# Forward V of heads 1 to 30 in one transfer per head, one product tile instead of two, V of head 30 kept for the backward

## The chip, the cores and the metric

The kernel runs on one core of a Trainium2 chip. The metric is the device time of one execution in microseconds (us). Engine names are those of the profile: PE is the matrix engine, PEld its weight loads, DVE the vector engine, ACT the scalar engine, POOL the general engine, SP the engine whose queue issues most transfers. A transfer is carried by 16 DMA engines, each with a share of its rows. The three runs of the kernel before lie within 3.2 us of each other.

## The reference

The forward is an adaptive layer norm block: an attention with one query token against a cache of 32 heads x 8192 keys x 192, and then a small mixer MLP, each gated by a modulation vector. The kernel computes the output and the gradients of nine inputs, the whole K and V cache among them.

```python
mod = silu(c) @ w_mod                       # six vectors of 640: sa, ca, ga, sb, cb, gb
h = layernorm(x) * (1 + ca) + sa
x = x + ga * attention(h, k_cache, v_cache, wq, wo)
h = layernorm(x) * (1 + cb) + sb
x = x + gb * mixer_mlp(h, w1, w2, w3, w4)

def attention(x, k, v, wq, wo):             # 1 token, 32 heads, 8192 keys, 192 wide
    q = (x @ wq) split in heads
    p = softmax(q . k * 192 ** -0.5)
    return (p . v, heads joined) @ wo

# returned: x, and by jax.vjp(grad_out) the gradients of
# x, k_cache, v_cache, wq, wo, w3, w4, c, w_mod
```

For a head with output gradient do, the backward needs dV = p x do (an outer product of 8192 x 192), dP = V . do, dS = p * (dP - c), and dK = dS x q (again an outer product).

## The kernel before, in words

**Tiles.** A head's K or V is laid out with 64 rows on each of the 128 partitions. It is handled in two halves, t = 0 and 1: a half tile is 128 partitions x 32 rows x 192 numbers of 2 bytes, that is 12288 bytes per partition, 1536 KB in all. Half tiles are what is loaded, multiplied and stored. Five half tiles (`big`) hold K in the forward and dK and dV in the backward. A pool `fv` of three half tiles holds the forward's V: half t of head h goes to slot (2h + t) mod 3. In the backward three more (`bv`, slots 3 to 5) join them to a ring of six.

**The forward** reads K and V once. For each head: `fwd_mult` (line 358; the multiplication itself is recorded at the helper's line 132) multiplies K by q on DVE into a product tile `prod` of the pool `fprod`; `fwd_ssum` (line 372) sums it over the head's width on PE into S_ps; `fwd_red`, `fwd_comb`, `fwd_max`, `fwd_exp` make the softmax numerators; `fwd_scale` makes EK = e * K, on ACT (line 407) and DVE (line 414), in four quarters; `fwd_kvA`, `fwd_kvB` (lines 432, 443; ps_a and ps_b) sum V against EK on PE, and `fwd_kvK` (line 449) sums EK alone. These moments are kept, so that the backward need not read K again.

The loop over i = 1 to 31 is a software pipeline with up to three heads in flight. The order of each engine is the order in which the program writes the work (`pin_order`); nothing is rescheduled. The steps of one iteration that the change touches, with the transfers among them:

```python
fwd_scale(i-1, 0); last quarter of kv(i-2); load V(i, 0); load wo of a pair (every second i)
fwd_ssum(i, 0); fwd_scale(i-1, 1); kv(i-1, 0); load K(i+1, 1); fwd_mult(i, 1)
fwd_scale(i-1, 2); kv(i-1, 1); load V(i, 1); fwd_ssum(i, 1); fwd_scale(i-1, 3)
reduction and kv(i-1, 2) in turn; fwd_exp(i); load K(i+2, 0); fwd_mult(i+1, 0)
```

All these loads stand in this order on SP's queue, and the 16 DMA engines work through them in that order. SP waits, load by load, for what frees the buffer: a V load for the PE sums that read the slot last, a K load for the scale steps on ACT and DVE. With two `prod` tiles, `fwd_mult(i, 1)` can write one while PE reads the other.

**The transition** after the loop finishes the attention's output, runs the MLP forward and backward, and gets the first do; its work is a chain over PE, DVE and ACT.

**The backward** runs from head 31 down to 0. `bwd_mult` (line 996) multiplies V by do in place, and PE sums it (line 1004); `bwd_dv` and `bwd_dk` write outer products to `big` tiles, and SP's queue stores them (lines 1012, 1039). V is read a second time through the ring (lines 737 to 786). V of head 31 and half 1 of head 30 are still there from the forward; V(30,0), V(29,0) and V(29,1) are loaded ahead, and each later load into a slot is issued when its last user is done. Five weight loads for wo stand in the same ring and go over POOL's queue (line 764). Towards the end the six ring slots, and two more, serve as extra tiles for stores (`tail_tiles`, line 1288).

Of the kernel before, what the change touches and what calls it, by code (L numbers as in the profile page):

```python
# [9 lines left out]
BF16 = mybir.dt.bfloat16  # L10
# [10 lines left out]
def kernel(  # L21
# [26 lines left out]
    nc = tc.nc  # L48

    def traced():  # L50
        return nc.cur_bb.bb.instructions
# [13 lines left out]
    P = 128  # L65
    D = A_x.shape[-1]
    _, HQ, S, DH = A_k_cache.shape
# [4 lines left out]
    JH = J // 2  # L72
# [58 lines left out]
    def mul(out, a, b):  # L131
        nc.vector.tensor_tensor(out=out, in0=a, in1=b, op=ALU.mult)  # L132
# [75 lines left out]
    V_hd = [A_v_cache[0, h].rearrange("(p j) d -> p j d", p=P) for h in range(HQ)]  # L208
# [16 lines left out]
    tail_tiles = {}  # L225

    def big_tile(name):
        k = big_order.pop(0)
        if isinstance(k, str):
            pool, tag = tail_tiles[k]  # L230
            return pool.tile([P, JH, DH], BF16, name=name, tag=tag)
        return big.tile([P, JH, DH], BF16, name=name, tag=f"big{k}")

    def load_k(h, t):
        tl = big_tile("K_sb")
        nc.sync.dma_start(out=tl, in_=K_hd[h][:, t * JH : (t + 1) * JH, :])
        return tl

    fpr_cm = tc.tile_pool(name="fprod", bufs=2)
    fpr = fpr_cm.__enter__()  # L240
    w0_cm = tc.tile_pool(name="w0", bufs=1, side="right")
    w0 = w0_cm.__enter__()
# [55 lines left out]
    def q_mm(g):  # L298
        for k in range(NQP):
            cc = g * NQP + k  # L300
            for i in range(NDC):
                nc.tensor.matmul(q_ps[:, cc : cc + 1], lhsT=wq_sb[g][:, i, k * P : (k + 1) * P], rhs=ha_bf[:, i : i + 1], start=(i == 0), stop=(i == NDC - 1), skip_group_check=True)  # L302
# [22 lines left out]
            return (0, P), (P, DH), 0, 3 * (h // 2), 3 * (h // 2) + 1  # L325
        return (DH - P, DH), (0, DH - P), DH - P, 3 * (h // 2) + 2, 3 * (h // 2) + 1

    def load_v(pool, h, t, slot, eng=None):
        tl = pool.tile([P, JH, DH], BF16, name="V_sb", tag=f"v{slot}")
        (eng or nc.sync).dma_start(out=tl, in_=V_hd[h][:, t * JH : (t + 1) * JH, :])  # L330
        return tl

    def load_fwd(h, t, kind):
        if not 0 <= h < HQ:
            return
        if kind == "v":
            st[h]["V"].append(load_v(fv, h, t, (2 * h + t) % 3))
        elif (h, t) not in K_st:
            K_st[h, t] = load_k(h, t)

# [2 lines left out]
    def pair_bc(pool, col_bf, hp, name, ps=None):  # L343
        t = pool.tile([P, 2 * DH], BF16, name=name, tag=name)
        bcast_cols(col_bf, 3 * hp, 3, t, act_copy, ps)
        return t
# [10 lines left out]
    def fwd_mult(h, t, st):  # L357
        if (h // 2) not in q_pb:
            q_pb[h // 2] = pair_bc(fsm, q_bf, h // 2, "q_pb")
        qh = q_pb[h // 2][:, (h % 2) * DH : (h % 2 + 1) * DH]  # L360
        prod = fpr.tile([P, JH, DH], BF16, name="prod")
        mul(prod, K_st[h, t], qh[:, None, :].to_broadcast([P, JH, DH]))
        st["prod"].append(prod)

# [181 lines left out]
            nc.vector.tensor_tensor_reduce(out=jk, in0=w4n(f, 0, D), in1=dbo_bc, scale=1.0, scalar=0.0, op0=ALU.mult, op1=ALU.add, accum_out=d_g[:, f : f + 1])  # L546

    st = {h: {"V": [], "prod": []} for h in range(HQ)}
    n_before = len(traced())
    fwd_mult(0, 0, st[0])  # L550
    first_ins = traced()[n_before]

# [14 lines left out]
    q_mm(1)  # L567
    q_mm(2)
    w0_cm.__exit__(None, None, None)
    fv = ctx.enter_context(tc.tile_pool(name="fv", bufs=1, side="right", reuse_waits="tile"))  # L570
    fwo = ctx.enter_context(tc.tile_pool(name="fwo", bufs=2, side="right", reuse_waits="tile"))
    mm_cm = tc.tile_pool(name="mm", bufs=1, side="right", reuse_waits="tile")
    mm = mm_cm.__enter__()
# [18 lines left out]
    for i in range(1, HQ):  # L592
        c, p, pp = 2 <= i < HQ, 0 <= i - 1 < HQ, 0 <= i - 2 < HQ
        n = i + 1 < HQ
# [132 lines left out]
    bv = ctx.enter_context(tc.tile_pool(name="bv", bufs=1, reuse_waits="tile"))  # L727
# [3 lines left out]
    w3T_t = tw.tile([P, JH, DH], BF16, name="w3T_t", tag="w3T_t").rearrange("p j d -> p (j d)")  # L731
    HS = list(range(HQ - 1, -1, -1))
    PS = list(range(HH - 1, -1, -1))
    V_b = {HS[0]: st[HS[0]]["V"], HS[1]: {1: st[HS[1]]["V"][1]}}
    wo_src = {(PS[k], cc): st[2 * PS[k] + 1]["wo"][:, cc, :] for k in range(2) for cc in range(3)}
    BATCHES = [(2, 3, 4), (5, 6, 7), (8, 9, 10), (11, 12, 13), (14, 15)]
    ring = []
    for i in range(1, HQ):
        ring += [("v", HS[i], t) for t in range(2) if (i, t) != (1, 1)]
        if i % 2 == 1 and 0 < i // 2 < len(BATCHES):  # L740
            ring.append(("w", i // 2, 0))
    ring_n, freed = [0], set()
    ldq = nc.sync
    NR = 6

    def ring_slot(n):
        return (3, 4, 5, 2, 0, 1)[n % NR]

    def ring_load():
        while ring_n[0] < len(ring) and (ring_n[0] < 3 or ring_key(ring_n[0] - NR) in freed):  # L750
            n = ring_n[0]
            kind, k, t = ring[n]
            slot = ring_slot(n)
            pool = bv if slot > 2 else fv
            ring_n[0] += 1
            if kind == "v":
                V_b.setdefault(k, {})[t] = load_v(pool, k, t, slot, ldq if n >= 3 else nc.sync)
            else:
                load_wo(k, pool.tile([P, JH, DH], BF16, name="V_sb", tag=f"v{slot}"))

    def load_wo(k, tl):
        lo, n = PS[BATCHES[k][-1]], len(BATCHES[k])
        tl = tl.rearrange("p j d -> p (j d)")[:, 0 : 3 * n * D].rearrange("p (c r) -> p c r", r=D)
        nc.gpsimd.dma_start(out=tl, in_=wo_v[:, 3 * lo : 3 * (lo + n), :])
        for hp in range(lo, lo + n):
            for cc in range(3):
                wo_src[hp, cc] = tl[:, 3 * (hp - lo) + cc, :]

    def ring_key(n):
        return ring[n] if n >= 0 else (("v", HS[0], 0), ("v", HS[0], 1), ("v", HS[1], 1))[n]  # L770

    ring_load()
    big_order[:] = [0, 4, 1, 4, 1, 2, 3, 4, 1, 2, 3, 4, 0, 1] + [2, 3, 4, 0, 1] * HQ
# [14 lines left out]
    def bwd_pf(h):  # L788
        bwd_pf_act(h)
        bwd_pf_dve(h)  # L790
# [146 lines left out]
    def fin_c_copy(lo, n, c_ps):  # L937
        dve_copy(c_bc[:, 2 * lo : 2 * (lo + n)], c_ps)
# [19 lines left out]
    def dq_last(h):  # L958
        for t in range(2):
            sum_rows(dql_ps, 0, K_st[h, t], [bst[h]["dS2"][:, j, 0:1] for j in range(t * JH, (t + 1) * JH)], h, False, t == 1)  # L960
# [18 lines left out]
    def bwd_dob(hp):  # L979
        do_pb[hp] = pair_bc(bsm, do_bf, hp, "do_pb")  # L980
        q_pb[hp] = pair_bc(bsm, q_bf, hp, "q_pb")
# [41 lines left out]
    def bwd_dv(h, t):  # L1023
        o = big_tile("dV")
        bwd_dv_act(o, h, t)
        bwd_dv_dve(o, h, t)
# [152 lines left out]
    for b, ks in enumerate(BATCHES):  # L1179
        units = [(PS[k], cc) for k in ks for cc in range(3)]  # L1180
        i = 1 + 2 * b
# [53 lines left out]
    for i in range(HQ):  # L1235
        h, nxt = HS[i], HS[i + 1] if i + 1 < HQ else None
        if i % 2 == 1 and nxt is not None:
            bwd_dob(nxt // 2)
        for f in J0[i]:
            f()  # L1240
        if i <= AHEAD:
            for t in range(2):
                bwd_mult(h, t, 2 if i == 0 else 1)
                if i == t == 0:
                    ring_load()
                    c_first = fin_c(PS[0], 1)
        ring_load()
        if i - 1 in dq:
            fin_dq(*dq.pop(i - 1))
        if i == 0:  # L1250
            fin_c_copy(PS[0], 1, c_first)
        if nxt is not None:
            if i > 0:
                bwd_pf(nxt)
            for t in range(0 if i > 0 else 1, 2):
                bwd_dv(nxt, t)
        if i < NPH:
            hook(i)
        if i == 3:
            bcast_cols(du_bf, 0, NFC, du_bc, act_copy)  # L1260
        for f in J1[i]:
            f()
        bwd_ds(h)
        if i == 0:
            dq_last(h)
        if i >= AHEAD and nxt is not None:
            for t in range(2):
                bwd_mult(nxt, t)
        bwd_dk(h, 0)
        bwd_dk(h, 1)  # L1270
        if i in cps:
            fin_c_copy(*cps.pop(i))
        if i == 1:
            mid_cols()
            job_mid()
            dve_copy(dmod_bf[:, 2 * NDC : 6 * NDC], dmod_c[:, 2 * NDC : 6 * NDC])
        if i == NPH - 1:
            fin_dq(*dq.pop(i))
            mm_cm.__exit__(None, None, None)
            for nm, b in (("in", 1), ("out", 4), ("bc", 1)):  # L1280
                side_cm.append(tc.tile_pool(name="side" + nm, bufs=b, side="right", reuse_waits="tile"))
                side[nm] = side_cm[-1].__enter__()
        for f in J2[i]:
            f()
        if i == I_SIDE:
            while side_cm:
                side_cm.pop().__exit__(None, None, None)
            xt = ctx.enter_context(tc.tile_pool(name="xt", bufs=1, side="right", reuse_waits="tile"))
            for k in "xy":
                tail_tiles[k] = (xt, "xt" + k)  # L1290
            for n in range(len(ring) - NR, len(ring)):
                slot = ring_slot(n)
                tail_tiles[f"v{n - len(ring) + NR}"] = (bv if slot > 2 else fv, f"v{slot}")
            big_order[:] = tail_list(big_order[0:5] + ["x", "y"])
    pin_order(first_ins)

# [29 lines left out]
```

## Time and profile before

| what | value |
|---|---|
| runs | 1382.59, 1381.43, 1379.37 us; median 1381.43 |
| profiled execution | 1379.59 us, of which the span is 1377.8 |
| busy in the span | PE 860.8 us (62%), DVE 1070.5 (78%), ACT 946.8 (69%), POOL 21.5 |
| moved | 569.26 MB, 413 GB/s on average |
| V loads | 125 of 1536 KB, median 14.8 us from issue to landing |
| K loads | 64 of 1536 KB, median 14.2 us |
| forward loop | prod of head 2 starts at 65.2 us, the last ps_b ends at 542.3 us |
| transition | to about 606 us |
| backward | to the end |

The profile is of one execution. A busy share says how long an engine worked, not whether the end waited for it. The span is what the profiler saw from the first to the last instruction; the execution's own time is 1.8 us longer. The granted clock of PE is given in tenths of full speed. The share of the DMA engines is the mean over all 16.

### The profile page before, as it was taken

How to read it: one execution, taken by the hardware profiler on the slowest of the kernel's cores; microseconds unless marked ns; L12 is line 12 of the kernel's file. 1: busy time of each engine (PE TensorE's matmuls, PEld its weight loads, DVE VectorE, ACT ScalarE, POOL GpSimd, SP SyncE). 2: the span in 40 equal slices, each digit the busy share in tenths (PEclk: the TensorE clock that was granted, in tenths of full speed). 3: DMA queues.
4: the chain of work that ended last, by engine and by line, in shares of the span. 5: the costliest groups of instructions: out<-in, count | busy, mean ns of one | idle time of the engine just before them, and what ended most of it. 6: DMA issues, size and time to landing. Idle time of an engine off the chain costs nothing.

```text
span 1377.8 us, 28365 instructions
## 1 busy us (share of the span) xinstructions
PE 860.8 (62%) x11655; PEld 675.9 (49%) x11655; DVE 1070.5 (78%) x1273; ACT 946.8 (69%) x2586; POOL 21.5 (2%) x33
## 2 busy tenths in 40 slices
PE   3799999999999999748545653443344325324440
PEld 3577777777777777736434542322223223213330
DVE  3588787888788787899988986965868669679792
ACT  1388777887778785866676676766767676767770
POOL 0000000000000000000000000000000000000000
PEclk9899999999999999666666665666666767656665
DMA  9999999999999999899999999999999999999997
GB/s 392 416 417 418 420 418 421 414 419 418 405 421 419 403 420 387 337 367 413 419 418 419 427 429 425 425 427 423 426 426 423 428 422 415 425 425 422 428 428 319
DMA packets 71758, 569.26 MB, mean 413 GB/s; under 512 B 6796, under 2 KB 14476, under 8 KB 31436
## 3 DMA queue, kind: packets, MB, share of 16 engines
q1 hardware_dynamic: 67934, 550.73, 96.1%
q0 software_dynamic: 3664, 16.71, 3.0%
q8 instruction: 91, 1.49, 0.4%
q14 instruction: 39, 0.32, 0.1%
q10 hardware_dynamic: 30, 0.00, 0.0%
HBM read 341.51 MB, written 225.91 MB: 412 GB/s over the span
## 4 chain that ended last, share of the span: by engine, by line
DMA 37%; DVE 29%; PE 22%; ACT 6%; SPq 3%; issue 2%; DVEq 0%; ACTq 0%
DMA out_dram<-dV 24%; DVE prod L132 9%; PE ps_a L432 8%; DVE dK L987 5%; DVE V_sb L132 5%; DMA out_dram<-dK 4%; PE S_ps L372 4%; DMA V_sb<-in_A_v_cache_dram 3%; DMA K_sb<-in_A_k_cache_dram 3%; ACT dV L1009 3%; PE ps_b L443 3%; PE kb_ps L449 2%; DVE dV L987 2%; DVE V_sb L921 2%; DMA out_dram<-dw 2%
## 5 line engine op out<-in xcount | busy, mean ns | idle before, releaser
L1009 ACT ACTIVATE dV<-do_pb,PF 128x192 bf16<-128x192 bf16 x1246 | 435.8, 440 | 141.9 <-DMA out_dram<-dV 101.3
L1004 PE MATMUL dP_ps<-V_sb,ident_bf 128*128 128x256 bf16 (+1 forms) x1584 | 233.3, 322 | 212.0 <-DVE V_sb L132 212.0
L407 ACT ACTIVATE EK<-K_sb,E_f 128x192 bf16<-128x192 bf16 x992 | 351.1, 442 | 4.3 <-PE kb_ps L302 2.9
L1004 PEld LDWEIGHTS <-ident_bf 128*128 128x128 bf16 x1584 | 180.9, 117 | 264.2 <-issue 138.9
L987 DVE TENSOR_TENSOR dK<-dS,q_pb 128x6144 bf16<-128x6144 bf16 x64 | 212.9, 3354 | 26.2 <-DMA out_dram<-dK 15.6
L132 DVE TENSOR_TENSOR prod<-K_sb,q_pb 128x6144 bf16<-128x6144 bf16 x64 | 214.4, 3349 | 4.1 <-DMA K_sb<-in_A_k_cache_dram 4.1
L132 DVE TENSOR_TENSOR V_sb<-V_sb,do_pb 128x6144 bf16<-128x6144 bf16 (+1 forms) x66 | 212.0, 3253 | 0.0
L432 PE MATMUL ps_a<-EK,V_sb 128*128 128x193 bf16 x1984 | 195.1, 251 | 1.3 <-DMA V_sb<-in_A_v_cache_dram 1.3
L432 PEld LDWEIGHTS <-V_sb 128*128 128x128 bf16 x1984 | 167.8, 100 | 19.3 <-issue 12.7
L987 DVE TENSOR_TENSOR dV<-P2h,do_pb 128x2304 bf16<-128x2304 bf16 (+2 forms) x67 | 89.5, 1354 | 111.3 <-DMA out_dram<-dV 106.8
L414 DVE TENSOR_TENSOR EK<-K_sb,P2h 128x1536 bf16<-128x1536 bf16 x124 | 117.5, 948 | 0.0
L372 PE MATMUL S_ps<-prod,ident_bf 64*64 64x256 bf16 x3072 | 101.3, 280 | 11.5 <-DVE prod L132 11.5
L443 PE MATMUL ps_b<-EK,V_sb 128*64 128x193 bf16 x1984 | 107.7, 250 | 0.0
L372 PEld LDWEIGHTS <-ident_bf 64*64 64x64 bf16 x3072 | 86.5, 110 | 31.0 <-issue 26.9
L443 PEld LDWEIGHTS <-V_sb 128*64 128x64 bf16 x1984 | 80.8, 110 | 19.6 <-issue 15.9
L393 ACT ACTIVATE E_f<-sm_ps,negm 128x64 f32<-128x64 f32 x31 | 9.8, 315 | 103.9 <-DVE negm L391 103.9
L376 DVE TENSOR_REDUCE S<-S_ps 128x128 f32<-128x1024 f32 x32 | 39.2, 1224 | 47.7 <-PE S_ps L372 47.6
L1115 PEld LDWEIGHTS <-ident_bf 128*128 128x128 bf16 x112 | 15.2, 136 | 123.8 <-issue 122.9
L449 PE MATMUL kb_ps<-EK,hot_bf 128*32 128x384 bf16 x992 | 63.5, 333 | 0.0
L1115 PE MATMUL js_ps<-wq,ident_bf 128*128 128x480 bf16 x64 | 23.8, 557 | 53.3 <-DVE wq L132 53.3
L1115 PE MATMUL js_ps<-wm,ident_bf 128*128 128x400 bf16 x48 | 14.9, 494 | 48.7 <-DVE wm L132 48.7
L195 ACT CAST do_pb<-bc_ps 128x384 bf16<-128x384 f32 x15 | 7.1, 474 | 52.0 <-PE bc_ps L191 52.0
(259 smaller groups left out, 758.5 us busy)
## 6 DMA issues: line engine op xcount, KB each, us to landing
V_sb<-in_A_v_cache_dram SPq DMA_DIRECT2D x125, 1536.0 KB, 14.8
K_sb<-in_A_k_cache_dram SPq DMA_DIRECT2D x64, 1536.0 KB, 14.2
out_dram<-dK SPq DMA_DIRECT2D x64, 1536.0 KB, 24.0
out_dram<-dV SPq DMA_DIRECT2D x61, 1536.0 KB, 22.3
wq<-in_A_wq_dram SPq DMA_DIRECT2D x3, 2560.0 KB, 31.4
wo_t<-in_A_wo_dram SPq DMA_DIRECT2D x16, 480.0 KB, 14.3
out_dram<-dwo POOLq DMA_DIRECT2D x16, 480.0 KB, 8.9
wq<-in_A_wq_dram SPq DMA_DIRECT2D x4, 1920.0 KB, 23.7
```

The costliest lines, as they stand in the source:

```text
L132: nc.vector.tensor_tensor(out=out, in0=a, in1=b, op=ALU.mult)
L372: nc.tensor.matmul(st["S_ps"][c0 : c0 + 64, r, t * JH : (t + 1) * JH, :], lhsT=ident_bf[64 * r : 64 * r + 64, 64 * r : 64 * r + 64], rhs=p ...
L376: nc.vector.reduce_sum(out=st["S2"], in_=st["S_ps"], axis=AX.X)
L407: nc.scalar.activation(out=st["EK"][q][:, jj, 0:DH], in_=K_st[h, t][:, r * JQ + jj, :], func=ACT.Copy, scale=st["E_f"][:, j : j + 1])
L414: nc.vector.tensor_tensor(out=EK[:, NA:JQ, 0:DH].rearrange("p j (d r) -> p j d r", r=2), in0=K_st[h, t][:, r * JQ + NA : (r + 1) * JQ, :]. ...
L432: nc.tensor.matmul(st["A_ps"][:, 0:n], lhsT=V_sb[:, r * JQ + jj, a0:a1], rhs=EK[:, jj, 0:n], start=(q == 0 and jj == 0), stop=(q == 3 and ...
L443: nc.tensor.matmul(st["B_ps"][g : g + 64, 0:n], lhsT=V_sb[:, r * JQ + jj, b0:b1], rhs=EK[:, jj, 0:n], start=(q == 0 and jj < 2), stop=(q = ...
L449: nc.tensor.matmul(kb_ps[g : g + 32, 0 : 2 * DH], lhsT=hot_bf[:, HQ - 1 - h : 2 * HQ - 1 - h], rhs=EK[:, jj : jj + 2, 0:DH], start=(h == 0 ...
L987: nc.vector.tensor_tensor(out=o.rearrange("p j (d r) -> p j d r", r=2), in0=pairs[:, :, None, :].to_broadcast([P, n, NP2, 2]), in1=vec.rea ...
L1004: nc.tensor.matmul(bst[h]["dP_ps"][:, t * JH + r : t * JH + r + n, :], lhsT=ident_bf, rhs=V_sb[:, :, k * DS : (k + 1) * DS], start=(k == 0 ...
L1009: nc.scalar.activation(out=o[:, jj, :], in_=vec_of(do_pb, h), func=ACT.Copy, scale=bst[h]["PF"][:, t * JH + jj : t * JH + jj + 1])
L1115: nc.tensor.matmul(ps[:, 0 : NDC * W].rearrange("p (i w) -> p i w", w=W), lhsT=ident_bf, rhs=w[:, :, k * W : (k + 1) * W], start=(k == 0), ...
```

## The change

- The forward's V lives in one tile of four half tiles, `V_f`. Head h has the pair of slots 2 (h mod 2) and the next one.
- V of heads 1 to 30 is loaded by one transfer of 24576 bytes per partition, at the place in iteration i where the load of V(i,0) stood. The load at the place of V(i,1) is gone. Heads 0 and 31 keep two loads of a half each.
- The pool of `prod` has one tile instead of two. A second pool of one tile, `fprod2`, serves the first halves of heads 0 and 1 at the start and is then closed.
- V of head 30 is whole in its two slots when the backward starts, so V(30,0) isn't loaded again. The ring begins with head 29, two loads ahead instead of three; slots 4 and 5 are the ones outside of `V_f`. The order of the ring's slots is written anew, by which the first ring load of wo and that of V(27,0) change the slots that they wait for.

In the order of instructions PE, ACT and DVE have the same sequence as before. SP's queue has 30 forward loads and one backward load fewer; in one iteration it now issues V(i) whole, wo, K(i+1,1), K(i+2,0).

```diff
-    fpr_cm = tc.tile_pool(name="fprod", bufs=2)
+    fpr_cm = tc.tile_pool(name="fprod", bufs=1)
...
-    def load_v(pool, h, t, slot, eng=None):
-        tl = pool.tile([P, JH, DH], BF16, name="V_sb", tag=f"v{slot}")
-        (eng or nc.sync).dma_start(out=tl, in_=V_hd[h][:, t * JH : (t + 1) * JH, :])
+    v_mem = {}
+
+    def v_tile(slot):
+        if slot < 4:
+            return v_mem[0][:, slot * JH : (slot + 1) * JH, :]
+        return bv.tile([P, JH, DH], BF16, name="V_sb", tag=f"v{slot}")
+
+    def load_v(h, t, slot):
+        tl = v_tile(slot)
+        nc.sync.dma_start(out=tl, in_=V_hd[h][:, t * JH : (t + 1) * JH, :])
         return tl
...
         if kind == "v":
-            st[h]["V"].append(load_v(fv, h, t, (2 * h + t) % 3))
+            if 0 < h < HQ - 1:
+                if t == 0:
+                    slot = 2 * (h % 2)
+                    nc.sync.dma_start(out=v_mem[0][:, slot * JH : (slot + 2) * JH, :], in_=V_hd[h])
+                    st[h]["V"] = [v_tile(slot + k) for k in range(2)]
+            else:
+                st[h]["V"].append(load_v(h, t, 2 * (h % 2) + t))
...
-        prod = fpr.tile([P, JH, DH], BF16, name="prod")
+        prod = (fpr2 if h < 2 and t == 0 else fpr).tile([P, JH, DH], BF16, name="prod")
...
+    fpr2_cm = tc.tile_pool(name="fprod2", bufs=1, reuse_waits="tile")
+    fpr2 = fpr2_cm.__enter__()
...
+    fpr2_cm.__exit__(None, None, None)
     fv = ctx.enter_context(tc.tile_pool(name="fv", bufs=1, side="right", reuse_waits="tile"))
+    v_mem[0] = fv.tile([P, 4 * JH, DH], BF16, name="V_f")
...
-    V_b = {HS[0]: st[HS[0]]["V"], HS[1]: {1: st[HS[1]]["V"][1]}}
+    V_b = {HS[0]: st[HS[0]]["V"], HS[1]: dict(enumerate(st[HS[1]]["V"]))}
...
-    for i in range(1, HQ):
-        ring += [("v", HS[i], t) for t in range(2) if (i, t) != (1, 1)]
+    for i in range(2, HQ):
+        ring += [("v", HS[i], t) for t in range(2)]
...
-        return (3, 4, 5, 2, 0, 1)[n % NR]
+        return (4, 5, 2, 3, 0, 1)[n % NR]
...
-        while ring_n[0] < len(ring) and (ring_n[0] < 3 or ring_key(ring_n[0] - NR) in freed):
+        while ring_n[0] < len(ring) and (ring_n[0] < 2 or ring_key(ring_n[0] - NR) in freed):
...
-        return ring[n] if n >= 0 else (("v", HS[0], 0), ("v", HS[0], 1), ("v", HS[1], 1))[n]
+        return ring[n] if n >= 0 else (("v", HS[0], 0), ("v", HS[0], 1), ("v", HS[1], 0), ("v", HS[1], 1))[n]
```

More of the change, by code (lines that the diff above doesn't have):

```diff
@@ L229, in big_tile @@
         if isinstance(k, str):
+            if k[0] == "v":
+                return v_tile(tail_tiles[k])
             pool, tag = tail_tiles[k]
@@ L753, in ring_load @@
             slot = ring_slot(n)
-            pool = bv if slot > 2 else fv
             ring_n[0] += 1
             if kind == "v":
-                V_b.setdefault(k, {})[t] = load_v(pool, k, t, slot, ldq if n >= 3 else nc.sync)
+                V_b.setdefault(k, {})[t] = load_v(k, t, slot)
             else:
-                load_wo(k, pool.tile([P, JH, DH], BF16, name="V_sb", tag=f"v{slot}"))
+                load_wo(k, v_tile(slot))
     def load_wo(k, tl):
@@ L1291 @@
             for n in range(len(ring) - NR, len(ring)):
-                slot = ring_slot(n)
-                tail_tiles[f"v{n - len(ring) + NR}"] = (bv if slot > 2 else fv, f"v{slot}")
+                tail_tiles[f"v{n - len(ring) + NR}"] = ring_slot(n)
             big_order[:] = tail_list(big_order[0:5] + ["x", "y"])
```

## The prediction

> **What bounds the kernel now.** I read the page's slices first, then the table of windows, the waits, the DMA issues, and last the chain of waits and the timeline around a head. The slices:
>
> ```profile
> PEclk9899999999999999666666665666666767656665
> DMA  9999999999999999899999999999999999999997
> GB/s 392 416 417 418 420 418 421 414 419 418 405 421 419 403 420 387 337 367 413 419 418 419 427 429 425 425 427 423 426 426 423 428 422 415 425 425 422 428 428 319
> ```
>
> The DMA row is 9 in nearly every slice. The forward fills slices 1 to 16 (PEclk 9); two slices of 337 and 367 GB/s are the transition; then comes the backward. The windows (columns: stretch, length, PE, PEld, DVE, ACT, POOL busy, clock, DMA share, GB/s):
>
> ```profile
> 300.00:350.00 50.00, 48.45 (x867) 38.37 (x865) 42.22 (x64) 38.79 (x115) 0.00 (x0) 1.00 1.01 419
> 450.00:500.00 50.00, 46.62 (x828) 36.92 (x825) 39.04 (x62) 37.06 (x111) 0.00 (x0) 0.97 1.00 408
> 550.00:600.00 50.00, 33.02 (x550) 30.85 (x550) 43.96 (x95) 36.61 (x96) 1.14 (x1) 0.60 0.91 357
> 750.00:800.00 50.00, 25.91 (x155) 22.06 (x154) 42.60 (x57) 33.71 (x91) 1.51 (x2) 0.64 1.01 428
> ```
>
> In the forward two limits stand side by side: PE is busy 48.45 of 50 us and the DMA engines 50 of 50. The backward is DMA alone (PE 25.91, DMA 1.01). Between 550 and 600 DMA has room (0.91). Which forward limit ends last shows in the waits and in the chain around one of them (start, length, what):
>
> ```profile
> DVE prod L132 <- DMA K_sb<-in_A_k_cache_dram: 4.1, 6, 1.2
> ```
>
> ```profile
> 210.71 2.89 ACT EK L407 x8
> 213.61 14.44 DMA K_sb<-in_A_k_cache_dram
> 228.08 3.36 DVE prod L132
> 231.44 0.08 DVE ao_c L135
> 231.52 0.04 issue
> 231.56 0.38 PE sm_ps L476 x2
> 231.95 2.48 PE ps_a L432 x16
> ```
>
> K(12,1) is issued at 213.61, when ACT has released its buffer, lands 14.44 us later, and prod(12,1) starts on its landing. PE has then idled 2.05 us (timeline), and ps_a x16 takes 2.48 us where it usually takes 1.47.
>
> By the timeline's prod starts, PE repeats every 31.13 us per two heads (prod(.,0) at 240.41, 271.54, 302.67, 333.81). Three times the step is longer: by 2.6 us at 228.08, 2.1 at 354.70, 2.2 at 450.43. Each time K(even head,1) was late (DVE waited 0.89, 0.42, 0.68 us), and ACT's and PE's next steps ran longer by another 1.6 us, while the granted clock was 0.5 for one stretch of 3.4 us (232.0 to 235.4, and alike). prod(30,1) starts at 514.22; prod(4,1) at 102.42 plus 13 x 31.13 gives 507.1: the forward lost 7.1 us to late K.
>
> So the shares creep behind the compute and a hiccup sets them back. The load that binds is K(even,1): from issue to need it has 13.50 us (13.49 to 13.59 where nothing waited), K(odd,1) 16.1, K(.,0) 17 to 19, V(odd,0) 16.7, V(even,0) 18.4. The order of issue in one iteration (start, length, queue, line):
>
> ```profile
> 289.12 0.33 SPq L330 DMA_DIRECT2D V_sb<-in_A_v_cache_dram  x1
> 289.68 1.50 PE L372 MATMUL S_ps<-prod,ident_bf 64*64 64x256 bf16 x48 [0.15 <-DVE prod L132]
> 291.94 3.35 DVE L132 TENSOR_TENSOR prod<-K_sb,q_pb 128x6144 bf16<-128x6144 bf16 x1
> 293.05 0.33 SPq L236 DMA_DIRECT2D K_sb<-in_A_k_cache_dram  x1
> 298.00 0.33 SPq L330 DMA_DIRECT2D V_sb<-in_A_v_cache_dram  x1
> 298.58 0.33 SPq L236 DMA_DIRECT2D K_sb<-in_A_k_cache_dram  x1
> ```
>
> These are V(16,0), K(17,1), V(16,1) and K(18,0), in that order on SP's queue; where the head behind V is even, K follows V(i,0) by 4.07 us (274.37 to 278.44).
>
> **The change, part by part.**
>
> *Packets.* Each of the 16 engines carries 8 rows of a transfer. By the trace's packet records a row of 1280 bytes takes 55 ns, 2560 102, 4096 164, 6144 236, 7680 291, 12288 460: a straight line of 8 ns plus 0.0368 ns per byte. A row of 24576 is then 912 ns instead of 2 x 460, 8 ns less; 8 rows give 64 ns, and one 4-byte semaphore write of 9 ns goes: 73 ns per engine and head, 30 heads 2.2 us. Bounds: 0, if all of it goes per byte; the dear end is the 16384-byte instruction fetch of 1053 ns (64 ns per KB against 37), by which a row would cost 0.66 us more and 30 heads 158 us. I take -2.2 and keep 0: the rows on the line come from the same memory to the same memory, the fetch does not; the dear end I leave out of the range.
>
> A rule bears on this. The Trainium skill, "DMA: Bandwidth & Descriptors", section "Anatomy of one DMA", gives each DMA some 2.0 us beside its bytes; 30 fewer transfers would by that be worth an estimated 60 us. That holds for transfers laid end to end; here DMA shares of 1.01 show the fixed part hidden under the next transfer, so the trace speaks against it and the sum keeps 2.2.
>
> *Order in the queue.* V(i) now goes whole at the place of V(i,0), at the same release (PE's ps_b of head i-2). K(i+1,1), issued some 4 us behind it, finds one half tile more ahead: 8 x 460 + 9 = 3.69 us on every engine. K(i+2,0) finds nothing more, its V(i,1) merely moved. V itself lands 3.69 later than its first half did: when K(even,1) is just in time (landing 13.50 + 4.07 = 17.6 us after V's issue), V has landed 3.7 earlier, at 13.9, against a need at 16.7: no price. Early: K(4,1) needed at 102.42 would land at about 105.1, so the compute has to fall back 2.7 to 3.7 us between heads 3 and 6, and then keep the distance. At the end: K(30,1) landed at 513.73; now 513.73 + 3.69 - 2.2 = 515.2. Against 507.1 that is 8.1 us of delay instead of 7.1: +1.0 at least. A hiccup overshoots: before, the last left 0.49 us of margin; the margin can be up to the 1.65 us that a hiccup adds beyond its wait. So +1.0 to +2.7; without the packet gain +3.2 to +4.9. I take +1.8, the middle of the first, as the line of packets is the nearer row.
>
> The overshoot hangs on the clock. The trace has it drop after a 2.05 us idle; the Trainium skill, "TensorE: Matmul & The Clock Gate", section "Part 1: The HAM clock gate", puts the cold state after an idle window of about 3.4 us. By it short waits would be free and the sum +1.0; the measurement decides, and I keep the overshoot.
>
> *One prod buffer.* prod(h,1) must wait for the end of ssum(h,0) on PE. At head 16 ssum(16,0) ends at 291.18 and prod(16,1) starts at 291.94: 0.76 us of room; heads 4 and 10 have 0.75 and 0.80, odd heads 1.6 (276.44 to 278.03). Nothing queued on DVE behind prod(h,1) moves: 0. The cover is DVE's scale step of the head before; if it went, the wait would be the 0.15 us from DVE to PE in the row at 289.68, per head, 4.8 us over 32; the odd ones keep theirs, 2.4. Ends 0 and +4.8.
>
> *V of head 30 kept.* One load of 1536 KB goes from the backward's start: 3.7 us at 425 GB/s. It was issued at 541 to 545, had landed by 564.25, and is used at 595. The DMA engines idle about 4 us between 558 and 570, 0.9 at 580, 2.0 at 602 to 606: the time goes to idle, 0. Bounds -3.7 (if it freed a saturated stretch) and 0. What is late next there is the PE, DVE and ACT chain of the transition. Later ring loads stand at the same releases, except V(27,0) and the first wo load, which swap (issue 3.3 us later, 3.1 earlier, near 604): taken as 0, ends -1 and +1.
>
> *Issues.* SP issues 31 transfers fewer at 0.33 us; SP is mostly waiting (264.5 us on ps_b at line 330): 0. PE, DVE and ACT keep every instruction and order.
>
> From 606 on DMA carries the same bytes at about 425 GB/s, so a later forward end passes to the end one to one.
>
> **Sum:** -2.2 + 3.7 - 0.5 (margin that was there) + 0.8 (half an overshoot) = +1.8 us. The profiled execution took 1379.59 us (span 1377.8, 1.8 around it), giving 1381.4; it lies 1.84 under the median of 1381.43, so the median becomes 1383.2.
>
> **Rivals.**
>
> *Slower, the queue shift in full and more hiccups.* Packets give nothing, K(even,1) is late more often, and each lateness costs a clock window: +3.2 to +4.9, with one or two more overshoots of 1.65 us up to +8. For it: three hiccups in 30 heads before at a creep of only 0.45 us per pair, and 8 of the 16 shares lag by 2 to 5 us (V at 216.78 landed at 8.7 to 11.8 us on some, 13.0 to 15.0 on others). Against: the packets' line. Chance 0.33.
>
> *Faster, because long rows are cheaper than the line.* The place is V's row in the 16 engines, 240 rows each. Every 10 ns off a row is 2.4 us off the DMA stream, which the forward's end follows. The forecast stands at 912 ns and +1.8; to be faster by 2.8 us a row must come to 893 ns or less (19 ns x 240 = 4.6 us). For it: in the forward the 12288-byte rows have a mean of 470 ns beside their median of 460, so there are some 10 ns of waiting per row that half as many rows may halve, and DMA share is 1.01, so nothing else hides such a gain. Against: six sizes on one straight line. At 893 to 875 ns: -2.8 to -7.1, 1378.6 to 1374.3. The kept V(30,0), were it in a saturated stretch, would lie in the same place (-3.7). Chance 0.19.
>
> *Prod stalls.* If ssum(h,0) ends later than prod can start, 0.15 us and more per head: +2.4 to +4.8, on top of +1.8: 1385.6 to 1388.0. Against: 0.75 us of room. Chance 0.08. The Trainium skill, "Trainium Kernel Development and Optimization", section Best Practices, asks for double buffers to overlap; the room in the row makes one enough here.
>
> **How the numbers follow.** Forecast 0.40; slower rival 0.33; prod 0.08; faster 0.19. A measurement tells 0.2% (2.8 us): the forecast's +1.0 to +2.7 lies within it (1382.4 to 1384.1); both slow rivals lie beyond, and the fast one below. Same 0.40, slower 0.41, faster 0.19. The range leaves out a tenth on either side: 1377 (about half of the fast rival is below) to 1389 (the slow rival's end, 1381.4 + 8).
>
> **What would show it.** Packets of V near 912 ns; prod waits on K at heads 3 to 6 and clock 0.5 there; K(even,1) landing 3.7 us later after its issue; the last ps_b of the forward, ending at 542.3 before, 1 to 3 us later; no wait of prod on S_ps; about as much less DMA busy at 541 to 565 as one half tile; the end of the span later by what the forward is. Wrong would be: V rows far from 912 ns, PE waiting for V, DVE waiting for S_ps, or a backward that does not carry the shift.

## The result and the profile after

The changed kernel takes 1382.33 us (median of 22 runs, 1380.99 to 1384.74) against 1380.26 us of the kernel before (22 runs, 1378.77 to 1383.33): +2.07 us, a ratio of 1.0014 with a 95% interval of 1.0009 to 1.0020. The forecast was +1.8 us, with 1377 to 1389 as its range. The loss lies within the 0.2% that the prediction took as its bound, as forecast. The sum came out; two of its terms did not, as the experiments show. The profiled execution took 1381.24 us, with a span of 1379.5 against 1377.8.

The slices of the page of the changed kernel, as those shown of before:

```profile
PEclk9899999999999999566566665666666767666665
DMA  9999999999999999699999999999999999999997
GB/s 393 418 422 410 423 417 419 410 419 423 420 418 408 416 424 403 226 376 417 419 421 422 427 425 425 425 427 423 425 426 423 428 424 419 422 425 423 429 430 313
```

One slice is different in kind: the first of the transition moves 226 GB/s, where it was 337. The windows (columns as before: stretch, length, PE, PEld, DVE, ACT, POOL busy, clock, DMA share, GB/s):

```profile
300.00:350.00 50.00, 48.45 (x900) 38.36 (x899) 40.60 (x62) 38.30 (x114) 0.00 (x0) 1.00 1.00 419
450.00:500.00 50.00, 47.23 (x885) 37.70 (x882) 40.99 (x70) 39.32 (x117) 0.00 (x0) 1.00 1.01 419
550.00:600.00 50.00, 33.57 (x570) 31.24 (x567) 42.80 (x99) 34.97 (x91) 1.15 (x1) 0.60 0.73 278
750.00:800.00 50.00, 25.38 (x152) 21.21 (x151) 42.89 (x52) 34.33 (x93) 1.51 (x2) 0.64 1.01 424
```

Forward and backward are saturated as before; between 550 and 600 us the DMA share falls from 0.91 to 0.73. By the trace's packet records all DMA work takes 1365.0 us instead of 1373.2, 8.2 less: 3.7 for V(30,0) and 4.5 for the forward. The idle time between 550 and 620 us (the length of the stretch less the time that an engine's packets took in the mean) grows from 6.4 to 15.1 us, 8.7 more. As much as the change takes off the DMA engines comes back as idle time in the transition.

The chain of waits around head 4 (start, length, what):

```profile
85.92 2.88 ACT EK L422 x8
88.81 0.02 issue
88.82 15.54 DMA K_sb<-in_A_k_cache_dram
104.36 0.03 issue
104.39 0.02 DVEq L132
104.41 0.04 issue
104.45 3.36 DVE prod L132
107.81 0.09 DVE ao_c L198
107.90 0.04 issue
107.94 0.38 PE sm_ps L491 x2
108.33 1.84 PE ps_a L447 x16
```

K(4,1) lands 15.54 us after its issue, where it had 13.5 until its use: prod(4,1) starts at 104.45 instead of 102.42. The clock is then 0.5 from 109.07 to 112.48, which adds another 1.5 us: prod(6,1) starts at 137.11, 3.56 us later than before (133.55). The compute has fallen back by about a half tile between heads 3 and 6, as worked out. From there on the difference to the kernel before shrinks: +2.4 at prod(20,1), +0.5 at prod(30,1) (514.75 against 514.22). A last stretch at half clock, from 518.67 to 522.08, adds 1.6 us, and the forward's last ps_b ends at 544.45 instead of 542.33.

The two lines of the waits that were to change or not to change (engine, line, what it waited for; total, times, longest):

```profile
DVE prod L132 <- DMA K_sb<-in_A_k_cache_dram: 4.8, 7, 1.9
PE ps_a L447 <- DMA V_f<-in_A_v_cache_dram: 1.7, 1, 1.7
```

The longest wait for K is now 1.9 us, at head 4; PE waits for V once, as in the kernel before (1.3). No line shows prod waiting for S_ps.

### The profile page after: what moved, and what is told of

Same layout as the page of the kernel before. It is cut to its first block, busy times and chain, and to the rows that moved or that the text cites. A ratio compares the mean times of both kernels' runs of the same rounds, so it can differ in the third digit from the quotient of the medians.

```text
span 1379.5 us, 28313 instructions
## 1 busy us (share of the span) xinstructions
PE 865.9 (63%) x11655; PEld 680.5 (49%) x11655; DVE 1070.2 (78%) x1273; ACT 946.7 (69%) x2586; POOL 21.5 (2%) x33
## 3 DMA queue, kind: packets, MB, share of 16 engines
q8 instruction: 91, 1.49, 0.4%
## 4 chain that ended last, share of the span: by engine, by line
DMA 38%; DVE 27%; PE 22%; ACT 7%; SPq 3%; issue 2%; DVEq 0%; ACTq 0%
DMA out_dram<-dV 26%; DVE prod L132 9%; PE ps_a L447 8%; DVE dK L1005 5%; PE S_ps L387 4%; ACT dV L1027 4%; DMA out_dram<-dK 4%; DMA V_f<-in_A_v_cache_dram 3%; DMA K_sb<-in_A_k_cache_dram 3%; DVE V_f L132 3%; PE ps_b L458 3%; PE kb_ps L464 2%; DVE dV L1005 2%; DMA out_dram<-dw 2%; ACT EK L422 2%
## 5 line engine op out<-in xcount | busy, mean ns | idle before, releaser
L1027 ACT ACTIVATE dV<-do_pb,PF 128x192 bf16<-128x192 bf16 x1166 | 408.0, 440 | 142.7 <-DMA out_dram<-dV 105.3
L1022 PE MATMUL dP_ps<-V_f,ident_bf 128*128 128x256 bf16 (+1 forms) x1080 | 161.4, 327 | 161.8 <-DVE V_f L132 161.8
L447 PE MATMUL ps_a<-EK,V_f 128*128 128x193 bf16 x1984 | 194.8, 251 | 1.8 <-DMA V_f<-in_A_v_cache_dram 1.7
L447 PEld LDWEIGHTS <-V_f 128*128 128x128 bf16 x1984 | 167.3, 100 | 19.7 <-issue 10.1
L1005 DVE TENSOR_TENSOR dV<-P2h,do_pb 128x2304 bf16<-128x2304 bf16 (+3 forms) x63 | 84.2, 1354 | 112.4 <-DMA out_dram<-dV 108.2
L132 DVE TENSOR_TENSOR V_f<-V_f,do_pb 128x6144 bf16<-128x6144 bf16 (+1 forms) x45 | 142.6, 3208 | 0.0
L458 PE MATMUL ps_b<-EK,V_f 128*64 128x193 bf16 x1984 | 108.8, 252 | 0.0
L1022 PE MATMUL dP_ps<-V_sb,ident_bf 128*128 128x256 bf16 x504 | 77.1, 329 | 44.5 <-DVE V_sb L132 44.5
L458 PEld LDWEIGHTS <-V_f 128*64 128x64 bf16 x1984 | 81.7, 110 | 19.7 <-issue 16.1
L132 DVE TENSOR_TENSOR V_sb<-V_sb,do_pb 128x6144 bf16<-128x6144 bf16 x21 | 69.6, 3350 | 0.0
```

The costliest lines, as they stand in the source:

```text
L447: nc.tensor.matmul(st["A_ps"][:, 0:n], lhsT=V_sb[:, r * JQ + jj, a0:a1], rhs=EK[:, jj, 0:n], start=(q == 0 and jj == 0), stop=(q == 3 and ...
L458: nc.tensor.matmul(st["B_ps"][g : g + 64, 0:n], lhsT=V_sb[:, r * JQ + jj, b0:b1], rhs=EK[:, jj, 0:n], start=(q == 0 and jj < 2), stop=(q = ...
L1005: nc.vector.tensor_tensor(out=o.rearrange("p j (d r) -> p j d r", r=2), in0=pairs[:, :, None, :].to_broadcast([P, n, NP2, 2]), in1=vec.rea ...
L1022: nc.tensor.matmul(bst[h]["dP_ps"][:, t * JH + r : t * JH + r + n, :], lhsT=ident_bf, rhs=V_sb[:, :, k * DS : (k + 1) * DS], start=(k == 0 ...
L1027: nc.scalar.activation(out=o[:, jj, :], in_=vec_of(do_pb, h), func=ACT.Copy, scale=bst[h]["PF"][:, t * JH + jj : t * JH + jj + 1])
```

## The experiments

Each ratio is to runs of the kernel before on the same chip, with its 95% interval. Where the end of the forward is told, it is the end of the last ps_b in the one trace of that kernel.

**1. Halves at their old places.**

```diff
-            if 0 < h < HQ - 1:
-                if t == 0:
-                    slot = 2 * (h % 2)
-                    nc.sync.dma_start(out=v_mem[0][:, slot * JH : (slot + 2) * JH, :], in_=V_hd[h])
-                    st[h]["V"] = [v_tile(slot + k) for k in range(2)]
-            else:
-                st[h]["V"].append(load_v(h, t, 2 * (h % 2) + t))
+            st[h]["V"].append(load_v(h, t, 2 * (h % 2) + t))
```

> This takes the changed kernel and puts V of heads 1 to 30 back as two half loads at their two old places in the iteration; one product tile, four V slots, V(30,0) kept and the ring of the changed kernel all stay. Theory (the order in the queue costs, the long rows give, all else is nothing): both the +3.7 us and the gain of the long rows go, so the time is that of the kernel before, 0 +-0.8 us, a ratio of 0.9994 to 1.0006; waits of prod on K back to some 4 us, first one at head 8 or later. Rival A (the one product tile or the ring of the backward costs the 2 us): the time stays at the changed kernel's, +2 us, a ratio of 1.0014.

Measured: 1.0015 (1.0006 to 1.0023). The forward did what the theory says: it ends at 542.30 us (before 542.33), and after those of the first 60 us the first wait for K is at head 12. But the kernel is as slow as the changed one. So something outside of the forward costs about as much as the whole result, and the order and the rows, which are those of the kernel before, have no part in it.

**2. Halves together.**

```diff
-                    nc.sync.dma_start(out=v_mem[0][:, slot * JH : (slot + 2) * JH, :], in_=V_hd[h])
-                    st[h]["V"] = [v_tile(slot + k) for k in range(2)]
+                    st[h]["V"] = [load_v(h, k, slot + k) for k in range(2)]
```

> The changed kernel with V(i) as two transfers of 12288 bytes per partition, one right behind the other, at the place where the whole V is issued: the order in the queue stays, the long rows go. Theory: the trace of the changed kernel has a mean of 927 ns for a row of 24576 bytes and 470 ns for one of 12288, so 13 ns per row and 240 rows per engine, 3.1 us, are lost: 2.1 + 3.1 = +5 us against the kernel before, a ratio of 1.0031 to 1.0044, with the last ps_b of the forward near 547 us; as delays come in steps of a clock window, +-1 us. Rival B (the length of rows is worth nothing, the order alone makes the difference): +2 us, a ratio of 1.0014, as the changed kernel.

Measured: 1.0045 (1.0033 to 1.0058), 1385.58 us, the forward ending at 546.97. The theory's +5 us lies in the interval, rival B's does not. From the halves at their old places to here only the order changes: 1.0015 to 1.0045, 4.1 us by the medians; the prediction's terms for it are 3.7 - 0.5 + 0.8 = 4.0. From here to the whole V only the rows change: 1.0045 to 1.0014, some 4 us; the packet records of the changed kernel give 927 ns (mean; median 915) for a row of 24576 bytes against 470 for 12288, 13 ns per row, 3.1 us over 240 rows.

**3. One product tile alone.**

```diff
-    fpr_cm = tc.tile_pool(name="fprod", bufs=2)
+    fpr_cm = tc.tile_pool(name="fprod", bufs=1)
...
-        prod = fpr.tile([P, JH, DH], BF16, name="prod")
+        prod = (fpr2 if h < 2 and t == 0 else fpr).tile([P, JH, DH], BF16, name="prod")
```

> The kernel before with one product tile instead of two (with the second pool for the first halves of heads 0 and 1), nothing else. Theory: prod(h,1) has 0.75 us of room behind the PE sums of the first half, so 0 +-0.7 us, a ratio of 0.9995 to 1.0005, and no wait of prod on S_ps in the waits. Rival A: +2 us, a ratio of 1.0014, with waits of prod on PE.

Measured: 1.0004 (0.9995 to 1.0013), and no wait of prod on S_ps. The room of 0.75 us is enough; rival A falls.

**4. V(30,0) once more.**

```diff
+    nc.sync.dma_start(out=V_b[HS[1]][0], in_=V_hd[HS[1]][:, 0:JH, :])
     ring_load()
```

> The changed kernel, with V(30,0) loaded once more into its own slot right before the two loads of V of head 29, so that the 1536 KB that the change saves are moved again. Theory: the DMA engines have 13 us of idle time between 550 and 606 in the changed kernel, the load fits in there: the time of the changed kernel, +2 us, a ratio of 1.0010 to 1.0018, and the DMA share of 550 to 600 rises from 0.73 to about 0.80. Rival C (the saved load counts, and hides a larger loss): +2.1 + 3.7 = +5.8 us, a ratio of 1.0042.

Measured: 1.0030 (1.0018 to 1.0041), between the two expectations. The window shows the load lying in idle time:

```profile
550.00:600.00 50.00, 34.79 (x574) 32.29 (x572) 42.45 (x99) 34.64 (x90) 1.15 (x1) 0.57 0.82 315
```

The share is 0.82 (0.73 in the changed kernel); the first dP of the backward starts at 589.7 (589.4). Of the 2.6 us by which the span is longer than the changed kernel's, 2.3 come after that, in a backward almost without idle time. By this run alone the saved load seemed to be worth some 2 us; experiment 11 says otherwise.

**5. The changed kernel with PE's gap filled.**

```diff
             fwd_ao((i - 4) // 2, st[i - 3]["wo"], st[i - 1]["sm"])
+            for _ in range(10):
+                nc.tensor.matmul(st[i - 1]["sm"][:, 424:512], lhsT=ident_bf, rhs=ident_bf[:, 0:88], start=True, stop=True)
```

> The changed kernel with ten small matmuls without use (128 x 88, into a part of the bank that nobody reads) put on PE between the attention's output step and the sum of the row sums, where PE idles 1.07 us in every second head. [...] Theory (what a late K costs beyond its wait is this clock window, and the forward's end is otherwise set by the landing of K): no window at half clock between 90 and 540 us unless K is over 0.6 us late; the 1.6 us of the window at 518.67 go: the changed kernel minus 1.6 to 2.3 us, a ratio to the kernel before of 0.9998 to 1.0005. Rival D (idle in the gap isn't what halves the clock): as the changed kernel, 1.0014.

Measured: 1.0015 (1.0006 to 1.0024). A miss: two stretches at half clock instead of four, and none near the end, but the time stays. The chain near the end of the forward says why:

```profile
501.37 13.86 DMA K_sb<-in_A_k_cache_dram
515.23 0.03 issue
515.26 0.02 DVEq L132
515.28 0.04 issue
515.32 3.36 DVE prod L132
```

K(30,1) lands at 515.23, and prod(30,1) starts on it. The prediction had worked out 515.2 for this landing. Where PE loses no time to its clock, the load is what it waits for here; so the reading is that the clock's stretches are spent, in the main, on time that a late K would have taken.

**6. The kernel before with the gap filled**, by the same lines.

> The kernel before with the same ten matmuls in the same gap. Theory (the forward is bound by DMA, and a clock window only brings forward a delay that later K loads would have asked for): no windows at half clock; only the margin of 0.5 us that K(30,1) had at the end is won, 0 to -1 us, a ratio of 0.9993 to 1.0000. Rival E (every clock window is lost for good): three windows of 1.65 us, -5 us, 0.9964.

Measured: 0.9998 (0.9989 to 1.0006), the forward ending at 542.40. This doesn't test rival E. The ten matmuls shorten the idle time in the gap from 1.07 to 0.65 us, but the clock is still halved in two stretches, from 263.61 and from 389.90, and the second is of 6.83 us: 10.24 us in all, as in the three stretches of the kernel before. Experiment 8 does test it.

**7. A sixth tile for K.**

```diff
-    big_order = [0, 1, 2, 3, 4] * 2 * HQ
+    big_order = ([0, 1, 2, 3, 4, "f"] * 11)[:64] + [4, 0, 1]
...
+    tail_tiles["f"] = (fpr, "bigf")
...
-        prod = fpr.tile([P, JH, DH], BF16, name="prod")
+        prod = fpr.tile([P, JH, DH], BF16, name="prod", tag="bigf" if h < 2 and t == 0 else "prod")
...
+    load_fwd(2, 1, "k")
...
-        load_fwd(i + 1, 1, "k")
+        load_fwd(i + 2, 0, "k")
...
-        load_fwd(i + 2, 0, "k")
+        load_fwd(i + 2, 1, "k")
```

> The kernel before with one product tile, and the place so won given to K instead of V: six half tiles of K in the forward, each K load issued half an iteration earlier in the same place of the code, V in three slots as before, the backward unchanged. Theory (K(even,1) binds, with 13.5 us from issue to need; with a sixth tile it has some 21, and V(odd,0) with 16.7 binds next, 3 us later): the forward's lag behind the transfers shrinks from 7 to 4 us, the last ps_b comes at about 539 us instead of 542.3, and the end with it: -2 to -4 us, a ratio of 0.9971 to 0.9986. Rival F (the DMA engines are never idle in the forward, so loads issued earlier land no earlier): 0.

Measured: 1.0002 (0.9993 to 1.0011), the forward ending at 543.20. A miss. prod no longer waits for K after head 1, yet nothing is won. The likely reason is my own arithmetic of the queue, which I had left out here: with K one half tile further ahead, each V load finds one half tile more in front of it, 3.69 us, and V(odd,0) had only 3 us more room than K(even,1).

**8. Six K tiles and the gap filled**, by the lines of 5 and 7.

> The kernel with six K tiles and the ten matmuls in PE's gap. Theory: as with six K tiles alone, less what is left of clock windows at the end: -3 to -5 us, a ratio of 0.9964 to 0.9978, no window at half clock in the forward. Rival F: 0 to -1 us.

Measured: 1.0007 (0.9998 to 1.0016), the forward ending at 542.59, with no stretch at half clock between 90 and 540 us. The waits of this kernel show what binds instead:

```profile
PE ps_a L433 <- DMA V_sb<-in_A_v_cache_dram: 8.6, 9, 1.8
```

PE now waits nine times for V. Eight of these waits lie after the first 60 us, 6.8 us together; in experiment 7 it was two with 0.8 us, beside four stretches at half clock of 1.6 us each. So the time that the clock no longer takes is taken by late loads of V: four stretches less bring the forward's end 0.6 us forward, and no gain in the whole. By rival E of experiment 6, every stretch lost for good, it would have been some 6 us, so that rival falls here. In experiments 6 to 8 and in the kernel before, the forward ends between 542.3 and 543.2 us, filled or not and with five tiles for K or six.

The last four experiments separate what experiment 1 had left over. The one thing of the backward that I had priced at nothing "with ends -1 and +1" was the swap of V(27,0) and the first wo load. SP's timeline shows it, first of the kernel before, then of the changed one (start, length, queue, line):

```profile
603.68 0.34 SPq L330 DMA_DIRECT2D V_sb<-in_A_v_cache_dram  x1
604.12 4.69 SPq L1012 DMA_DIRECT2D out_dram<-dV  x2
```

```profile
607.62 0.34 SPq L339 DMA_DIRECT2D V_f<-in_A_v_cache_dram  x1
608.06 2.87 SPq L1030 DMA_DIRECT2D out_dram<-dV  x2
```

The dV store stands behind V(27,0) on SP's queue. Against the forward's end V(27,0) is issued at +61.4 us before and at +63.2 after, and this lies where the DMA engines have idle time. In all traces it is +63.1 to +64.4 us in the six kernels with the swap and +60.3 to +61.5 in the eight without.

**9. The changed kernel with the swap undone.**

```diff
-        return (4, 5, 2, 3, 0, 1)[n % NR]
+        return (4, 5, 2, 3, 1, 0)[n % NR]
...
-        return ring[n] if n >= 0 else (("v", HS[0], 0), ("v", HS[0], 1), ("v", HS[1], 0), ("v", HS[1], 1))[n]
+        return ring[n] if n >= 0 else (("v", HS[0], 0), ("v", HS[0], 1), ("v", HS[1], 1), ("v", HS[1], 0))[n]
```

> The changed kernel with one thing of its ring put back: the first wo load of the ring waits for V(30,1) again and V(27,0) for V(30,0), as in the kernel before. In the traces V(27,0) and the dV store behind it on SP's queue are issued at 603.7 and 604.1 before and at 607.6 and 608.1 in the changed kernel, where 2.1 us of the 3.9 are the forward's. Theory S (the 1.8 us by which SP holds the store back lie where the DMA engines are idle, so they are lost): the changed kernel minus 1 to 1.8 us, a ratio to the kernel before of 1.0002 to 1.0008. Rival N (the swap is nothing; what the backward loses is chance or the one tile of V): as the changed kernel, 1.0014.

Measured: 1.0013 (1.0004 to 1.0023). By itself this doesn't tell S from N.

**10. The swap alone**, in the kernel before.

```diff
-        return (3, 4, 5, 2, 0, 1)[n % NR]
+        return 3 if n == 0 else (1, 4, 5, 2, 0, 3)[n % NR]
...
-        while ring_n[0] < len(ring) and (ring_n[0] < 3 or ring_key(ring_n[0] - NR) in freed):
+        while ring_n[0] < len(ring) and (ring_n[0] < 3 or ring_key({5: 0, 6: -1}.get(ring_n[0], ring_n[0] - NR)) in freed):
```

> The kernel before with the swap alone: the first wo load of the ring goes to the slot of V(30,0) and V(27,0) to that of V(30,1). Theory S: +1 to +1.8 us, a ratio of 1.0007 to 1.0013. Rival N: 0, 0.9995 to 1.0005.

Measured: 1.0003 (0.9994 to 1.0012): both expectations lie in the interval. The trace shows the place all the same. V(27,0) and the store are held back by 2.9 us, and the DMA share of 600 to 612 us is 0.75 where it was 0.83 (first the kernel before, then this one):

```profile
600.00:612.00 12.00, 6.52 (x42) 4.84 (x39) 11.83 (x17) 10.85 (x29) 1.80 (x2) 0.78 0.83 292
```

```profile
606.57 0.34 SPq L330 DMA_DIRECT2D V_sb<-in_A_v_cache_dram  x1
607.01 1.70 SPq L1012 DMA_DIRECT2D out_dram<-dV  x2
```

```profile
600.00:612.00 12.00, 6.54 (x41) 4.72 (x39) 11.83 (x17) 10.75 (x29) 1.81 (x2) 0.78 0.75 277
```

**11. The forward of the change alone**: the lines of 4 and of 9.

> The forward of the changed kernel alone: V(30,0) is loaded again ahead of V of head 29, and the swap in the ring is undone, so that the backward moves the bytes of the kernel before at the same releases. Theory S: what is left is the forward, whose last ps_b came 2.1 us later in the changed kernel's trace (544.5 against 542.3): +1 to +2.2 us, a ratio of 1.0007 to 1.0016; the run with V(30,0) loaded again and the swap in place was 1.0030. Rival N: 1.0030 again.

Measured: 1.0011 (1.0001 to 1.0020), where rival N had 1.0030. And 9, which has V(30,0) kept and is otherwise this kernel, is 1.0013: V(30,0) kept is worth nothing that shows.

**12. Halves at their old places, and the swap undone**: the lines of 1 and of 9.

> The kernel with V as halves at the two old places (one product tile, four V slots, V(30,0) kept), with the swap undone as well. Its forward ended at 542.3 us as that of the kernel before, yet it was slower by 1.0015. Theory S: without the swap 0 to +0.8 us, a ratio of 1.0000 to 1.0006. Rival N: 1.0015 again.

Measured: 0.9998 (0.9990 to 1.0007), where rival N had 1.0015: the time of the kernel before is back, with one product tile, four V slots and V(30,0) kept.

**What the four pairs say together.** With the swap and without it (ratio to the kernel before):

| kernel | swap | no swap |
|---|---|---|
| whole V, V(30,0) kept | 1.0014 | 1.0013 |
| whole V, V(30,0) loaded again | 1.0030 | 1.0011 |
| halves at their old places, V(30,0) kept | 1.0015 | 0.9998 |
| the kernel before | 1.0003 | 1 |

The four differences are 0.0001, 0.0019, 0.0017 and 0.0003, in the mean 0.0010 or 1.4 us. A single one is uncertain by about 0.0013 (two intervals of 0.0009), their mean by about 0.0006. From the end of the forward to the end of the span the traces have 835.0 to 837.5 us in the six kernels with the swap (changed, 1, 2, 4, 5, 10; mean 836.6) and 834.1 to 836.4 in the eight without (before, 3, 6, 7, 8, 9, 11, 12; mean 835.0). The ranges overlap, and the changed kernel's own trace has the lowest of the six, 835.0, where the kernel before has 835.5.

The idle time of the DMA engines shows the swap more sharply. Between 598 and 625 us it is, by the packet records and counted as above:

| kernel | swap | no swap |
|---|---|---|
| whole V, V(30,0) kept | 1.49 us | 0.64 us |
| whole V, V(30,0) loaded again | 1.48 us | 0.63 us |
| halves at their old places, V(30,0) kept | 1.52 us | 0.37 us |
| the kernel before | 2.87 us | 1.87 us |

In each pair the swap makes 0.9 to 1.2 us more. (Of the eight kernels without it, seven have 0.4 to 0.7; why the kernel before has 1.87 stays open.) So about 1 us of the swap's mean price is seen where it arises; the times of the pairs, 0.1 to 2.6 us, scatter around it.

For the forward, whole V against halves, the four differences are -0.0001 and 0.0015 with V(30,0) kept, 0.0027 and 0.0011 with it loaded again: 0.0013 in the mean or 1.8 us, uncertain by 0.8. (The last two also change the product tile, 1.0004 by experiment 3.) In the traces the forward ends at 544.45, 544.57, 543.17 and 545.58 us with the whole V (changed, 4, 9, 11; mean 544.4) and between 542.19 and 543.39 with halves at the old places (before, 1, 3, 10, 12; mean 542.6), again 1.8 us apart. So in the mean over the pairs the forward costs 1.8 us and the swap 1.4. The two add up to 3.2, and the changed kernel itself has 2.07 (1.2 to 2.8); undoing the swap in it won 0.0001, uncertain by 0.0013. How its own 2.07 us divide is not shown. No version here beats the kernel before by more than a measurement tells.

## Why the prediction was right, and where it was not

- *Order in the queue, +4.0 net of margin and overshoot.* Shown: 4.1 us between experiments 1 and 2, where nothing else changes. The early place was shown too: K(4,1) landed 15.54 us after its issue, waits at heads 3 and 4, half clock right after. The end was not reached as worked out: K(30,1), put at 515.2, came at 515.23 in experiment 5, but in the changed kernel prod(30,1) starts at 514.75 without a wait for it, 0.5 us later than before, and the other 1.6 us of the forward's 2.1 are the last stretch at half clock. So in this trace the forward's size came out by another path than the one worked out, and that is luck.
- *Packets, -2.2.* The mechanism was right, the term mis-sized: the quick rows are as forecast (the tenth percentile is 912 ns), but the mean gains 13 ns and not 8, which is 3.1 us, and experiment 2 and the changed kernel are some 4 us apart (4.3, uncertain by about 2). The faster rival's argument (half as many rows, half of the waiting) had something to it, though far from enough for its price.
- *Half an overshoot, +0.8.* Not borne out. In experiments 5 and 8 the filled gap took away two of four and four of four stretches at half clock; the forward ended 1.0 and 0.6 us earlier, and the time did not change by anything that can be told. I had treated what the clock costs beyond a wait as lost; by these two runs it is mostly delay that the next late load would have brought.
- *The swap in the ring, 0 with ends -1 and +1.* This is the step that failed. I had the releases (3.3 us later, 3.1 earlier) and called them even; but I did not name what stands behind V(27,0) on SP's queue, the dV store, and I counted the idle time of the DMA engines at 602 to 606 us for V(30,0) alone. Against the forward's end V(27,0) is issued 1.8 us later in the changed kernel and 3.0 in experiment 10. In the mean of the four pairs it costs about 1.4 us (0.6 to 2.2), of which about 1 us is seen as idle time of the DMA engines; the end I had kept was +1. That the sum came out although one term was mis-sized, one not borne out and one left at nothing is in part luck: the mean prices of forward and swap would make 3.2 us.
- *One prod, 0.* Right (experiment 3); so is the room read from the trace.
- *V of head 30 kept, 0.* Right: experiments 9 and 11 differ by 0.0002, and the freed time shows as a DMA share of 0.73. Experiment 4, 1.0030, doesn't fit to this by itself; with the swap undone the difference is gone. Why the swap seems to cost more there than in the changed kernel stays open: the DMA engines idle no more for it near 604 us (0.85 us in both pairs).
- *From 606 on one to one.* Right in the mean; but from the start of the dP of head 29 to the end the fourteen traces have 743.9 to 747.3 us, for 311.9 to 312.4 MB that are left there, so that one trace's backward can hide or double an effect of this size.

## What to carry to other kernels

In a kernel bound by transfers, time taken off the DMA engines is worth something only where work waits for the transfers behind it. Here the longer rows took some 3 us off a stretch whose K loads were late, and experiment 2 without them was some 4 us slower; the 3.7 us of V(30,0) lay ahead of a chain of PE, DVE and ACT work, and became idle time. For loads in one queue, a deeper buffer for one of two streams can push the other back, as six tiles for K did with V here, so count both needs against the same order. When two releases change places, price what stands behind each waiting transfer on its queue, above all where the engines have idle time.

## What the runs showed of the hardware

In the forward loop PE's clock is halved in stretches of 3.41 us, or of two such steps, that lie on one grid: the stretches of a run start a whole number of 3.41 us apart (in the kernel before 231.97, 358.27 and 453.84, that is 37 and 28 steps). They need no late load. With six K tiles (experiment 7) prod waits for no K after head 1 and the clock still halves, here at 138.24, after the usual idle of 1.06 us (PE's timeline):

```profile
137.75 0.38 PE L477 MATMUL sm_ps<-rowsum,ones_mat_f 128*128 128x2 f32 x2 [1.06 <-DVE ao_c L135]
138.00 2.56 PE L433 MATMUL ps_a<-EK,V_sb 128*128 128x193 bf16 x16
```

It does so at 138.24, 264.53, 390.82 and 486.40, and each such stretch delays the next head by 1.6 us. Most idles of 1.07 us are followed by no such stretch. Nor are all longer ones: in experiment 3 a step of the grid with 1.55 us of idle, in experiment 1 one with 1.45 and in experiment 5 one with 1.43 have none after them. Where the idle lies in the step may decide, but no run here settles it. The Trainium skill, "TensorE: Matmul & The Clock Gate", section "Part 1: The HAM clock gate", has the free-running window of this length, which the grid bears out, and the cold state after an idle window; here about a third of a window of idle was enough, 1.06 us of 3.41.

A row of 24576 bytes takes 915 ns at the median and 927 in the mean, two rows of 12288 in the same stretch (90 to 520 us, kernel before) 928 and 939: the longer row is cheaper by more than the straight line through the shorter ones gave.
